# Cached sliding-window attention: twelve instead of eight rows of each wo head on five DMA engines, and other code blocks on two engines

## The chip, the cores and the metric

The kernel runs on one core of one Trainium2 chip. Its time is the device time of one execution in microseconds (us). Besides the plain runs there is one execution under the hardware profiler, whose span, from the first to the last instruction of the program, is a little shorter than the time reported for it.

## The reference

One decoding step of grouped-query attention over the last 512 positions of a cache: 32 batch rows, 32 query heads on 8 key/value heads, head size 128, bf16.

```python
W = min(4096, max(256, Sk // 4))                     # 512
q = (x @ wq).reshape(B, Sq, Hq, Dh)                  # x 32x512, wq 512x4096
k = jnp.repeat(k_cache[:, :, Sk - W:, :], rep, axis=1)
v = jnp.repeat(v_cache[:, :, Sk - W:, :], rep, axis=1)
scores = jnp.einsum("bhqd,bhkd->bhqk", q, k) * (Dh ** -0.5)
o = jnp.einsum("bhqk,bhkd->bhqd", softmax(scores), v)
out = o.reshape(B, Sq, Hq * Dh) @ wo                 # wo 4096x512
```

The window of K and that of V are 33.6 MB each, wq and wo 4.2 MB each: 75.5 MB in all, each byte read once.

## The kernel before, in words

**Tiling.** The 32 batch rows are taken in 8 quads of 4. A quad's K is one transfer of 4 MB into `K_sb[q % 2]` (128 partitions, one for each batch row, key/value head and quarter of the window; 32 KB each), its V the same into `V_sb[q % 2]`, for the last three quads in two pieces. `wq` is first loaded into `V_sb[1]`. At the end most of `wo` goes into `K_sb[0]`.

**wo in two parts.** The output projection is a sum over 32 heads of 128 rows each. The first `4 * NI` = 120 rows of every head are laid out over 128 partitions (32 heads by 4 groups of `NI` = 30 rows) and loaded by the steps W0, W1 and W2 of `LOADS` (line 269), 20, 8 and 2 rows of each partition at a time (`WOP`); each such transfer is carried by all sixteen DMA engines, eight partitions each. The last `NX` = 8 rows of every head go, one head to a partition, into another tile, `wx_row`, which lies over `QT_sb`. These are the steps A0 to A3 (line 262): 20, 5, 5 and 2 heads (`HEADS`), as transfers whose outer size is 5, 5, 5 and 2, and that many engines carry them. A head of A is 8 KB; a partition of W0, W1 and W2 is 20, 8 and 2 KB.

**The order of the work** is written out by hand: `PE_OPS`, `DVE_OPS` and `ACT_OPS` list the steps of TensorE, VectorE and ScalarE, `LOADS` those of the SP queue, and each step waits for the ends that `needs` gives. SP issues all large loads in one order, K and V of the quads in turn, then A0 to A3, then W0 to W2, then half of the store. A load of K waits until the transposes of the quad two before (T) are done, a load of V until the matmuls of the quad two before (P) are done with that part, A for the step Z0, W for T6.1.

**The steps of a quad.** T turns K into `KT_sb` on VectorE (L491), in two halves w = 0 and 1. S are the score matmuls (L353) with `QBD`, a block-diagonal copy of the queries, as weights. GpSimd makes `QBD` for a quad in four copies (L312), one of the two buffers at a time, after S of the quad two before. M and N (VectorE) and X (ScalarE) are the softmax. E (L368) spreads the probabilities over rows by matmuls with selectors `E_sb`, one 128 x 128 selector for each of 16 combinations, which GpSimd fills at the start in four copies (L301). G and B build the weights `bd` of P, the 128 matmuls with V (L383). C evicts their result into `C_sb`. F (L395, weights `F_sb`) and H (L404, weights `F_ext`) sort it into rows for the projection: F for the first 120 rows of each head, evicted by D (ScalarE, L561) into `o_sel`, H for the last eight, evicted by U (L566) into `o_ext`. `F_sb` and `F_ext` are zeroed by GpSimd and filled by VectorE in eight small copies (L471, L474) at the start.

**Z0** (ScalarE, L572) writes zeros over `wx_row` before A loads into it, since only 32 of its 64 partitions get a head.

**The end.** After D7 TensorE does the matmuls of W0 (20 x 4, L421), those of the head rows (8 x 4, L435), W1 and W2. VectorE and ScalarE each evict half of the result, and SP and ScalarE store it.

**Where the code lies.** TensorE's program has a directive ahead of its first matmul (line 320, `addr_align(256, offset=178)`): the next instruction stands at slot 178 of a block of 256 instructions, and the slots skipped are filled with instructions that do nothing. No other engine has one.

Of the kernel before, what the change touches and what calls it, by code (L numbers as in the profile page):

```python
# [5 lines left out]
BF16 = mybir.dt.bfloat16  # L6
# [14 lines left out]
P2.12.32 F2 H2 S4.0 S4.1 P3.0.12 E4 P3.12.32 S5.0 S5.1 S6.0 P4.0.4 E5 P4.4.8 S6.1 P4.8.24 E6 P4.24.32  # L21
F3 H3 S7.0 P5.0.20 S7.1 P5.20.32 E7 F4 H4 P6.0.32 F5 H5 P7.0.32 F6 H6 F7 H7
"""
# [6 lines left out]
X0 X1 G0 B0.4.8 G1 B1.4.8 C0.0.4 D0 U0 X2 G2 B2.4.8 C1.0.4 D1 U1 X3 G3 B3.4.8 C2.0.4 D2 U2 X4 G4 B4.4.8  # L30
C3.0.2 X5 G5 B5.4.8 X6 G6 C4.0.2 B6.4.7 D3 U3 B6.7.8 Z0 X7 C5.0.2 G7 B7.5.6 D4 U4 B7.6.8 C6.0.2 D5 U5 C7.0.2
D6 U6 D7 U7
"""
# [6 lines left out]
V_PIECES = 5 * [[0, 32]] + 2 * [[0, 16, 32]] + [[0, 18, 32]]  # L40
WOP = [(0, 20), (20, 28), (28, 30)]
HEADS = [(0, 20, 4, 0), (20, 25, 1, 32), (25, 30, 1, 33), (30, 32, 1, 34)]


# [4 lines left out]
def bass_standalone__sliding_block_cached__sampling_kernel(  # L49
# [15 lines left out]
    P = 128  # L65
# [4 lines left out]
    R = W // KB  # L70
    NI = 30
    NX = DH - 4 * NI
# [57 lines left out]
    with ExitStack() as es:  # L130
# [17 lines left out]
        F_ext = sb("F_ext", [P, 64], F32)  # L148
        E_sb = sb("E_sb", [P, KB, REP, 32, KB], BF16)
        F_sb = sb("F_sb", [P, 4, HQ, 4], F32)  # L150
        mask = sb("mask", [P, HKV], F32)
# [7 lines left out]
        wo_sb = K_sb[0][:, 0:NI * D].rearrange("p (i n) -> p i n", i=NI)  # L159
        wx_row = QT_sb[0:64].rearrange("p j w h t -> p (j w h t)")  # L160
        wx_sb = wx_row.rearrange("p (i n) -> p i n", i=NX)
# [10 lines left out]
        m_red = spare[:, 1856:1920].bitcast(F32)  # L172
        out_sb = P_bf[0:64, 0:256].rearrange("p (c n) -> p c n", c=2)
        Q_row = KT_sb[:, 0].rearrange("p r c t -> p (r c t)")[:, 0:HD]

# [3 lines left out]
        def folds(q):  # L179
# [10 lines left out]
            "pe_xT pe_q pe_Y dve_xT dve_q dve_QT dve_m dve_r dve_c act_q act_warm out_y "  # L190
            "pool_x pool_e pool_ei pool_q pool_f pool_m pool_j pool_qbd pool_fz"
        ).split()
# [10 lines left out]
        for b0, b1 in X_PARTS:  # L203
# [5 lines left out]
            V_sb[1][:, :], wq.rearrange("(p k) n -> p (k n)", k=DKT)  # L209
        ).then_inc(sem_wq, 16)  # L210
        regions = es.enter_context(ExitStack())
        block = regions.enter_context(nc.Block())
# [26 lines left out]
        def _(sp):  # L239
# [3 lines left out]
            for op in ops_of(" ".join(LOADS)):  # L243
# [14 lines left out]
                elif kind == "A":  # L258
                    wait([ends["Z", 0]])
                    h0, h1, k, p0 = HEADS[q]  # L260
                    n = (h1 - h0) // k
                    sp.dma_start(  # L262
                        wx_row[p0:p0 + 4 * n:1 if k == 4 else 4, :],
                        wo_h[h0:h1, 4 * NI * D:].rearrange("(k j) m -> j k m", k=k),
                    ).then_inc(sem_wx, 16)
                else:
                    wait([ends["T", NQ - 2, 1]])
                    i0, i1 = WOP[q]
                    sp.dma_start(  # L269
                        wo_sb[:, i0:i1, :].rearrange("p i n -> p (i n)"),  # L270
                        wo_r[:, :, i0 * D:i1 * D],
                    ).then_inc(sem_wo[q], 16)
# [3 lines left out]
        def _(pool):  # L276
            wait = Waits(pool)

            def diag(t, pattern, name):
# [11 lines left out]
            diag(m_id[:, :, :, :], [[-32, 4], [-4, HKV], [-1, KB]], "pool_m")  # L291
            pool.memset(F_sb[:, :, :, :], 0.0).then_inc(s["pool_fz"], 1)
            pool.memset(F_ext[:, :], 0.0).then_inc(s["pool_fz"], 1)

            diag(E_id[:, :, :].rearrange("p e (b h) -> p e b h", b=4),
                 [[-1, REP], [-4, 4], [-16, HKV]], "pool_ei")
            pool.memset(E_sb[:, :, :, :, :], 0.0).then_inc(s["pool_e"], 1)
            pool.wait_ge(s["pool_e"], 1)
            pool.wait_ge(s["pool_ei"], 2)
            for k in range(KB):  # L300
                pool.tensor_copy(E_sb[:, k, :, :, k], E_id[:, :, :]).then_inc(s["pool_e"], 1)  # L301
            pool.wait_ge(s["pool_e"], 5)
            pool.wait_ge(s["pool_q"], 1)
            pool.wait_ge(s["dve_QT"], 1)
            for q in range(NQ):
                if q >= 2:
                    wait([ends["S", q - 2, 1]])
                for b in range(4):
                    pr = slice(32 * b, 32 * b + 32)
                    if q or b:  # L310
                        pool.wait_ge(s["pool_qbd"], 4 * q + b)
                    pool.tensor_copy(  # L312
                        QBD[pr, q % 2].rearrange("p (w t) (h c) -> p w t h c", w=2, h=HKV)[
                            :, :, :, :, 4 * b:4 * b + 4],
                        QT_sb[pr, q].rearrange("p w (h e) t -> p w t h e", h=HKV),
                    ).then_inc(s["pool_qbd"], 1)

        @block.tensor
        def _(pe):
            pe.addr_align(256, offset=178)  # L320
            wait = Waits(pe)
# [20 lines left out]
            def scores(q, w):  # L342
                if w == 0:
                    pe.wait_ge(s["pool_qbd"], 4 * q + 4)
                if q == 0 and w == 0:
# [64 lines left out]
            for op in orders["PE"]:  # L410
                wait(needs(op))
                run[op[0]](*op[1:]).then_inc(op_sem["PE", op[0]], 1)
            wait([ends["D", NQ - 1]])
            for j, (i0, i1) in enumerate(WOP):
                pe.wait_ge(sem_wo[j], 16)
                last = j == len(WOP) - 1
                for cs in ((0, 1), (2, 3)) if last else (range(4),):
                    for i in range(i0, i1):
                        for c in cs:
                            n = 2 * (c % 2) + c // 2  # L420
                            ins = pe.matmul(  # L421
                                Y_ps[32 * c:32 * (c + 1), 0:P],
                                lhsT=o_sel[:, i, :],
                                rhs=wo_sb[:, i, n * P:(n + 1) * P],
                                start=i == 0, stop=i == NI - 1, tile_position=(0, 32 * c),
                            )
                    if last:
                        ins.then_inc(s["pe_Y"], 1)
                if j == 0:
                    wait([ends["U", NQ - 1]])  # L430
                    pe.wait_ge(sem_wx, 16 * len(HEADS))
                    for i in range(NX):
                        for c in range(4):
                            n = 2 * (c % 2) + c // 2
                            pe.matmul(  # L435
                                Y_ps[32 * c:32 * (c + 1), 0:P],
                                lhsT=o_ext[:, i, :],
                                rhs=wx_sb[:, i, n * P:(n + 1) * P],
                                start=False, stop=False, tile_position=(0, 32 * c),
                            )  # L440

# [8 lines left out]
        def _(dve):  # L450
# [27 lines left out]
            for n in range(4):  # L478
# [48 lines left out]
        def _(act):  # L527
# [41 lines left out]

            def zero(_):  # L570
                act.wait_ge(s["pool_qbd"], 4 * NQ)
                return act.activation(  # L572
                    wx_row, junk[0:64, 0:1].to_broadcast([64, NX * D]), ACTF.Copy
                )
# [40 lines left out]
```

## Time and profile before

| | us |
|---|---|
| plain runs, median of 3 (lowest to highest) | 184.67 (184.37 to 184.73) |
| the profiled execution, its own time | 184.59 |
| its span | 183.3 |
| VectorE busy, share of the span | 106.7, 58% |
| TensorE matmuls busy, share of the span | 120.4, 66% |
| ScalarE busy | 54.2, 30% |
| GpSimd busy | 17.1, 9% |
| mean rate of all DMA over the span | 414 GB/s |
| mean granted TensorE clock | 0.842 of full speed |

How to read it: the page names an engine, a source line and tiles ("out<-in") for each group of instructions, and for the DMA the queue. q1 is the queue of SP's loads, q10 that of ScalarE's, q8 and q14 bring instructions. "Busy" of a DMA queue is the time that its packets took, as a share of sixteen engines over the span. The chain of work that ended last is followed back from the last instruction, at each step to what released it. The trace behind the page also holds every DMA packet (queue, start, length, bytes), and every increment of a semaphore by a DMA engine; a transfer over sixteen engines makes sixteen of these as its engines finish.

### The profile page before, as it was taken

The numbers are of one execution on the slowest core, as the hardware profiler recorded it, in microseconds if no ns is written. First come the engines' busy times: TensorE is split into PE (matmuls) and PEld (weight loads), VectorE is DVE, ScalarE is ACT, GpSimd is POOL, SyncE is SP. The second block draws the span as 40 slices with busy tenths as digits, with TensorE's granted clock in tenths as the row PEclk, the third lists the DMA queues.
The fourth block names the chain that finished last, engine by engine and source line by source line (L and its number), as shares of the span: only waits on it lengthen the run. The fifth ranks groups of instructions, "written<-read, shape, count | busy, mean of one in ns | idle before, by whom it ended". The sixth has DMA issues, their size and how long they took to land.

```text
span 183.3 us, 3870 instructions
## 1 busy us (share of the span) xinstructions
PE 120.4 (66%) x1676; PEld 58.0 (32%) x1676; DVE 106.7 (58%) x109; ACT 54.2 (30%) x101; POOL 17.1 (9%) x53
## 2 busy tenths in 40 slices
PE   0029802416779699429944995440799978999984
PEld 0013300002535344304520252000255433655463
DVE  0042399998569534973289326999825994703030
ACT  3001300010590527501650135001053693803040
POOL 7900013020200020002000200001000000000000
PEclk9999995555769999996995599655559999999999
DMA  6998999989999999999999999999999999999981
GB/s 234 459 443 386 429 458 454 422 386 451 458 443 383 429 454 447 415 401 451 442 429 415 424 442 440 408 429 451 436 408 404 426 426 429 432 418 427 436 359 62
DMA packets 3517, 75.80 MB, mean 414 GB/s; under 512 B 429, under 2 KB 525, under 8 KB 653
## 3 DMA queue, kind: packets, MB, share of 16 engines
q1 hardware_dynamic: 3409, 75.52, 96.5%
q8 instruction: 13, 0.21, 0.5%
q10 hardware_dynamic: 92, 0.05, 0.1%
q14 instruction: 3, 0.02, 0.0%
HBM read 75.53 MB, written 0.03 MB: 412 GB/s over the span
## 4 chain that ended last, share of the span: by engine, by line
DMA 65%; DVE 19%; PE 8%; issue 4%; SPq 3%; ACT 0%; DVEq 0%
DMA K_sb<-in_k_cache_dram 32%; DVE KT_sb L491 16%; DMA V_sb<-in_v_cache_dram 16%; DMA K_sb<-in_wo_dram 11%; DMA V_sb<-in_wq_dram 7%; PE ps L336 5%; PE ps L383 2%; DVE QT_sb L483 2%; SPq L262 2%; SPq L255 1%; PE ps L421 1%; PE ps L353 1%; DVE C_sb L516 0%; SPq L269 0%; ACT KT_sb L533 0%
## 5 line engine op out<-in xcount | busy, mean ns | idle before, releaser
L491 DVE STREAM_TRANSPOSE KT_sb<-K_sb 128x4096 f32<-128x4096 f32 x16 | 70.5, 4430 | 7.2 <-DMA K_sb<-in_k_cache_dram 7.1
L383 PE MATMUL ps<-V_sb,bd 32*128 32x512 bf16 x1024 | 64.0, 402 | 4.4 <-DMA V_sb<-in_v_cache_dram 2.1
L353 PE MATMUL ps<-KT_sb,QBD 128*32 128x512 bf16 x256 | 24.7, 522 | 35.2 <-DVE KT_sb L491 26.0
L383 PEld LDWEIGHTS ps<-V_sb,bd 32*128 32x128 bf16 x1024 | 27.7, 98 | 37.8 <-issue 14.1
L353 PEld LDWEIGHTS ps<-KT_sb,QBD 128*32 128x32 bf16 x256 | 6.4, 111 | 50.4 <-DVE KT_sb L491 31.3
L539 ACT ACTIVATE P_f<-ps,negmax 128x512 f32<-128x512 f32 x8 | 5.5, 687 | 56.8 <-DVE negmax L499 56.8
L557 ACT ACTIVATE C_sb<-ps 32x512 f32<-32x512 f32 x22 | 12.9, 588 | 24.4 <-PE ps L383 24.2
L552 ACT ACTIVATE bd<-PTc,mask 128x512 bf16<-128x512 bf16 x31 | 20.1, 712 | 0.3
L312 POOL COPY QBD<-QT_sb 32x128 bf16<-32x128 bf16 x32 | 9.3, 289 | 106.3 <-PE ps L353 87.2
L511 DVE TENSOR_SCALAR bd<-PTc,mask 128x512 bf16<-128x512 bf16 x33 | 9.4, 349 | 14.0 <-ACT PTc L546 14.0
L516 DVE COPY C_sb<-ps 32x512 f32<-32x512 f32 x10 | 6.9, 693 | 13.9 <-PE ps L383 13.8
L395 PE MATMUL ps<-C_sb,F_sb 128*128 128x120 f32 x64 | 9.2, 286 | 6.8 <-ACT C_sb L557 6.5
L497 DVE TENSOR_REDUCE maxv<-ps 128x1 f32<-128x512 f32 x8 | 5.5, 687 | 10.8 <-PE ps L353 10.7
L395 PEld LDWEIGHTS ps<-C_sb,F_sb 128*128 128x128 f32 x64 | 7.7, 191 | 9.6 <-ACT C_sb L557 8.4
L368 PE MATMUL ps<-P_bf,E_sb 128*128 128x128 bf16 x128 | 9.9, 239 | 1.0 <-DVE P_bf L505 1.0
L336 PE MATMUL ps<-V_sb,bd 128*128 128x512 bf16 x32 | 9.0, 451 | 2.0 <-DMA V_sb<-in_wq_dram 2.0
L546 ACT ACTIVATE PTc<-ps 128x512 bf16<-128x512 f32 x8 | 4.7, 593 | 18.3 <-PE ps L368 18.3
L368 PEld LDWEIGHTS ps<-P_bf,E_sb 128*128 128x128 bf16 x128 | 8.4, 108 | 4.9 <-DVE P_bf L505 2.8
L325 PE MATMUL ps<-bd 32*128 32x128 bf16 x4 | 0.6, 298 | 10.5 <-DMA bd<-in_x_dram 10.5
L533 ACT ACTIVATE KT_sb<-ps 128x512 bf16<-128x512 f32 x4 | 2.4, 597 | 17.0 <-PE ps L336 17.0
L453 DVE CAST bd<-ps 128x512 bf16<-128x512 f32 x1 | 0.7, 692 | 11.2 <-PE ps L325 11.2
L480 DVE CAST KT_sb<-ps 128x512 bf16<-128x512 f32 x4 | 2.8, 692 | 6.0 <-PE ps L336 6.0
(37 smaller groups left out, 44.1 us busy)
## 6 DMA issues: line engine op xcount, KB each, us to landing
K_sb<-in_k_cache_dram SPq DMA_DIRECT2D x8, 4096.0 KB, 24.6
V_sb<-in_v_cache_dram SPq DMA_DIRECT2D x5, 4096.0 KB, 28.7
V_sb<-in_v_cache_dram SPq DMA_DIRECT2D x4, 2048.0 KB, 20.6
V_sb<-in_wq_dram SPq DMA_DIRECT2D x1, 4096.0 KB, 12.3
K_sb<-in_wo_dram SPq DMA_DIRECT2D x1, 2560.0 KB, 17.6
V_sb<-in_v_cache_dram SPq DMA_DIRECT2D x1, 2304.0 KB, 14.2
V_sb<-in_v_cache_dram SPq DMA_DIRECT2D x1, 1792.0 KB, 14.9
K_sb<-in_wo_dram SPq DMA_DIRECT2D x1, 1024.0 KB, 19.4
```

Of the source, the lines that this page charges most:

```text
L312: pool.tensor_copy(QBD[pr, q % 2].rearrange("p (w t) (h c) -> p w t h c", w=2, h=HKV)[:, :, :, :, 4 * b:4 * b + 4], QT_sb[pr, q].rearrange ...
L336: ins = pe.matmul(ps[:, n], lhsT=xT_sb[:, kt, :], rhs=wq_sb[:, kt, n * 512:(n + 1) * 512], start=kt == 0, stop=kt == DKT - 1, tile_positio ...
L353: ins = pe.matmul(S_ps[32 * c:32 * c + 32, :], lhsT=QBD[:, q % 2, 2 * w + t, c0:c0 + 32], rhs=KT_sb[:, w, :, KB * h:KB * h + KB, t], start ...
L368: ins = pe.matmul(EP_ps[:, e * R:(e + 1) * R], lhsT=E_sb[:, k, e].rearrange("p m j -> p (m j)"), rhs=P_bf[:, k * R:(k + 1) * R], start=k = ...
L383: ins = pe.matmul(O_ps[:, b, :], lhsT=bd[pr, q % 2, 4 * g:4 * g + 4].rearrange("p r h e -> p (r h e)"), rhs=V_sb[q % 2][pr, 512 * g:512 * ...
L395: ins = pe.matmul(folds(q), lhsT=F_sb[:, d].rearrange("p h d -> p (h d)"), rhs=C_sb[:, q % 2, :, NI * d:NI * d + NI], start=d == 0, stop=d ...
L491: return dve.transpose(KT_sb[:, w].bitcast(F32).rearrange("p r c t -> p r (c t)"), K_sb[q % 2][:, :].bitcast(F32).rearrange("p (r w c) -> ...
L497: dve.tensor_reduce(maxv[:, q:q + 1], S_ps, AX.X, ALU.max).then_inc(s["dve_m"], 1)
L511: ins = dve.tensor_scalar(o, i, m, None, op0=ALU.mult)
L516: ins = dve.tensor_copy(*pick_args(q, r))
L552: ins = act.activation(o, i, ACTF.Copy, scale=m)
L557: ins = act.activation(*pick_args(q, r), ACTF.Copy)
```

## The change

- `NI` goes from 30 to 29, and so `NX` from 8 to 12: W0, W1 and W2 carry 19, 8 and 2 rows of each partition, A0 to A3 twelve rows (12 KB) of each head. The transfers' outer sizes stay.
- `wx_row` lies over the first half of `KT_sb`. Z0 is gone from ScalarE; GpSimd zeroes `wx_row` in a memset after S7.0, the last reader of that half, and A waits for this.
- GpSimd makes `QBD` for two quads at once, in four copies of twice the size, after S of the quad before the two. `E_sb` holds one selector of 33 columns for each of 4 instead of 16 combinations, read at shifted places; GpSimd fills it in one copy. Filling `F_sb` and `F_ext` moves from VectorE to GpSimd (one copy and three), which waits for the reduction that makes `F_hd`. GpSimd's program goes from 75 to 59 instructions, VectorE's from 135 to 127 with the new directive.
- VectorE has a directive ahead of its part of the block: its next instruction stands at the start of a block of 128 slots, and it branches over the slots skipped. TensorE's directive has offset 154 instead of 178.
- In the order, H7 comes before F7 and U6 and U7 before D6 and D7. TensorE does the head rows' 48 matmuls first, after U7 and A, and then, after D7, those of W0, W1 and W2 (76, 32 and 8).

```diff
@@ -19,7 +19,7 @@
...
-F3 H3 S7.0 P5.0.20 S7.1 P5.20.32 E7 F4 H4 P6.0.32 F5 H5 P7.0.32 F6 H6 F7 H7
+F3 H3 S7.0 P5.0.20 S7.1 P5.20.32 E7 F4 H4 P6.0.32 F5 H5 P7.0.32 F6 H6 H7 F7
...
-C3.0.2 X5 G5 B5.4.8 X6 G6 C4.0.2 B6.4.7 D3 U3 B6.7.8 Z0 X7 C5.0.2 G7 B7.5.6 D4 U4 B7.6.8 C6.0.2 D5 U5 C7.0.2
-D6 U6 D7 U7
+C3.0.2 X5 G5 B5.4.8 X6 G6 C4.0.2 B6.4.7 D3 U3 B6.7.8 X7 C5.0.2 G7 B7.5.6 D4 U4 B7.6.8 C6.0.2 D5 U5 C7.0.2
+U6 D6 U7 D7
...
-WOP = [(0, 20), (20, 28), (28, 30)]
+WOP = [(0, 19), (19, 27), (27, 29)]
 HEADS = [(0, 20, 4, 0), (20, 25, 1, 32), (25, 30, 1, 33), (30, 32, 1, 34)]
+PICKS = [(0, 20, 4, 0), (20, 30, 2, 32), (30, 32, 1, 34)]
...
-    NI = 30
+    NI = 29
...
-        E_sb = sb("E_sb", [P, KB, REP, 32, KB], BF16)
-        F_sb = sb("F_sb", [P, 4, HQ, 4], F32)
+        E_sb = sb("E_sb", [P, REP, 33, KB], BF16)
+        F_pad = sb("F_pad", [P, 4 * (4 * HQ + 1)], F32)
...
-        wx_row = QT_sb[0:64].rearrange("p j w h t -> p (j w h t)")
+        wx_row = KT_sb[0:64, 0].rearrange("p r c t -> p (r c t)")[:, 0:NX * D]
...
+        F_sb = F_pad[:, 0:16 * HQ].rearrange("p (d h c) -> p d h c", d=4, h=HQ)
+        F_diag = F_pad[:, :].rearrange("p (d m) -> p d m", d=4)[:, :, 0:4 * HQ].rearrange(
+            "p d (h c) -> p d h c", c=4)[:, :, :, 0]
...
+        nc.vector.addr_align(128, offset=0, max_nops=0)
...
-                    wait([ends["Z", 0]])
+                    sp.wait_ge(s["pool_z"], 1)
...
-            pool.memset(F_sb[:, :, :, :], 0.0).then_inc(s["pool_fz"], 1)
+            pool.memset(F_pad[:, :], 0.0).then_inc(s["pool_fz"], 1)
...
-            pool.memset(E_sb[:, :, :, :, :], 0.0).then_inc(s["pool_e"], 1)
+            pool.memset(E_sb[:, :, :, :], 0.0).then_inc(s["pool_e"], 1)
             pool.wait_ge(s["pool_e"], 1)
             pool.wait_ge(s["pool_ei"], 2)
-            for k in range(KB):
-                pool.tensor_copy(E_sb[:, k, :, :, k], E_id[:, :, :]).then_inc(s["pool_e"], 1)
-            pool.wait_ge(s["pool_e"], 5)
+            pool.tensor_copy(E_sb[:, :, 0:32, KB - 1], E_id[:, :, :]).then_inc(s["pool_e"], 1)
+            pool.wait_ge(s["pool_e"], 2)
+            pool.wait_ge(s["pool_fz"], 2)
+            pool.wait_ge(s["dve_c"], 1)
+            pool.tensor_copy(
+                F_diag, F_hd.unsqueeze(1).to_broadcast([P, 4, HQ])
+            ).then_inc(s["pool_fz"], 1)
+            for h0, h1, k, p0 in PICKS:
+                n = (h1 - h0) // k
+                pool.tensor_copy(
+                    F_ext[:, p0:p0 + 4 * n].rearrange("p (j k) -> p k j", k=4)[:, 0:k],
+                    F_hd[:, h0:h1].rearrange("p (k j) -> p k j", k=k),
+                ).then_inc(s["pool_fz"], 1)
             pool.wait_ge(s["pool_q"], 1)
             pool.wait_ge(s["dve_QT"], 1)
-            for q in range(NQ):
-                if q >= 2:
-                    wait([ends["S", q - 2, 1]])
+            for q in range(0, NQ, 2):
+                if q:
+                    wait([ends["S", q - 1, 1]])
                 for b in range(4):
                     pr = slice(32 * b, 32 * b + 32)
                     if q or b:
-                        pool.wait_ge(s["pool_qbd"], 4 * q + b)
+                        pool.wait_ge(s["pool_qbd"], 2 * q + b)
                     pool.tensor_copy(
-                        QBD[pr, q % 2].rearrange("p (w t) (h c) -> p w t h c", w=2, h=HKV)[
-                            :, :, :, :, 4 * b:4 * b + 4],
-                        QT_sb[pr, q].rearrange("p w (h e) t -> p w t h e", h=HKV),
+                        QBD[pr].rearrange("p u a (h c) -> p u a h c", h=HKV).rearrange(
+                            "p u (w t) h c -> p (u w) t h c", w=2)[:, :, :, :, 4 * b:4 * b + 4],
+                        QT_sb[pr, q:q + 2].rearrange("p u w (h e) t -> p (u w) t h e", h=HKV),
                     ).then_inc(s["pool_qbd"], 1)
+            wait([ends["S", NQ - 1, 0]])
+            pool.memset(wx_row, 0.0).then_inc(s["pool_z"], 1)
...
-            pe.addr_align(256, offset=178)
+            pe.addr_align(256, offset=154)
...
-                    pe.wait_ge(s["pool_qbd"], 4 * q + 4)
+                    pe.wait_ge(s["pool_qbd"], 4 * (q // 2) + 4)
...
-                    pe.wait_ge(s["pool_e"], 5)
+                    pe.wait_ge(s["pool_e"], 2)
                 for e in range(REP):
+                    window = E_sb[:, e].rearrange("p m j -> p (m j)")
                     for k in range(KB):
                         ins = pe.matmul(
                             EP_ps[:, e * R:(e + 1) * R],
-                            lhsT=E_sb[:, k, e].rearrange("p m j -> p (m j)"),
+                            lhsT=window[:, KB - 1 - k:KB - 1 - k + P],
...
-                    pe.wait_ge(s["dve_c"], 7 + len(HEADS))
+                    pe.wait_ge(s["pool_fz"], 3 + len(PICKS))
...
+            wait([ends["U", NQ - 1]])
+            pe.wait_ge(sem_wx, 16 * len(HEADS))
+
...
+            for i in range(NX):
+                projected(o_ext[:, i, :], wx_sb[:, i], range(4), first=i == 0)
             wait([ends["D", NQ - 1]])
...
-                if j == 0:
-                    wait([ends["U", NQ - 1]])
-                    pe.wait_ge(sem_wx, 16 * len(HEADS))
-                    for i in range(NX):
...
 
...
-            dve.wait_ge(s["pool_fz"], 2)
...
-            for d in range(4):
-                dve.tensor_copy(F_sb[:, d, :, d], F_hd[:, :]).then_inc(s["dve_c"], 1)
-            for h0, h1, k, p0 in HEADS:
-                n = (h1 - h0) // k
-                dve.tensor_copy(
-                    F_ext[:, p0:p0 + 4 * n].rearrange("p (j k) -> p k j", k=4)[:, 0:k],
-                    F_hd[:, h0:h1].rearrange("p (k j) -> p k j", k=k),
-                ).then_inc(s["dve_c"], 1)
...
-            def zero(_):
-                act.wait_ge(s["pool_qbd"], 4 * NQ)
-                return act.activation(
-                    wx_row, junk[0:64, 0:1].to_broadcast([64, NX * D]), ACTF.Copy
-                )
-
             run = {"X": exponential, "G": gather, "B": spread, "C": pick, "D": folded,
-                   "U": folded_ext, "Z": zero}
+                   "U": folded_ext}
```

More of the change, by code (lines that the diff above doesn't have):

```diff
@@ L190, in bass_standalone__sliding_block_cached__sampling_kernel @@
             "pe_xT pe_q pe_Y dve_xT dve_q dve_QT dve_m dve_r dve_c act_q act_warm out_y "
-            "pool_x pool_e pool_ei pool_q pool_f pool_m pool_j pool_qbd pool_fz"
+            "pool_x pool_e pool_ei pool_q pool_f pool_m pool_j pool_qbd pool_fz pool_z"
         ).split()
@@ L412, in _, with projected @@
                 run[op[0]](*op[1:]).then_inc(op_sem["PE", op[0]], 1)
+            wait([ends["U", NQ - 1]])
+            pe.wait_ge(sem_wx, 16 * len(HEADS))
+            def projected(lhsT, rhs, cs, first=False, last=False):
+                for c in cs:
+                    n = 2 * (c % 2) + c // 2
+                    ins = pe.matmul(
+                        Y_ps[32 * c:32 * (c + 1), 0:P],
+                        lhsT=lhsT, rhs=rhs[:, n * P:(n + 1) * P],
+                        start=first, stop=last, tile_position=(0, 32 * c),
+                    )
+                return ins
+            for i in range(NX):
+                projected(o_ext[:, i, :], wx_sb[:, i], range(4), first=i == 0)
             wait([ends["D", NQ - 1]])
@@ L418, in _ @@
                     for i in range(i0, i1):
[L419 to L425, printed above, removed]
-                            )
+                        ins = projected(o_sel[:, i, :], wo_sb[:, i], cs, last=i == NI - 1)
                     if last:
                         ins.then_inc(s["pe_Y"], 1)
-                if j == 0:
-                    wait([ends["U", NQ - 1]])
-                    pe.wait_ge(sem_wx, 16 * len(HEADS))
-                    for i in range(NX):
[L433 to L440, printed above, removed]
         def spread_args(q, h):
@@ L568, in folded_ext @@
                     EP_ps[0:64, 0:4 * NX].rearrange("p (b i) -> p i b", b=4), ACTF.Copy)
-            def zero(_):
-                act.wait_ge(s["pool_qbd"], 4 * NQ)
-                return act.activation(
-                    wx_row, junk[0:64, 0:1].to_broadcast([64, NX * D]), ACTF.Copy
-                )
             run = {"X": exponential, "G": gather, "B": spread, "C": pick, "D": folded,
-                   "U": folded_ext, "Z": zero}
+                   "U": folded_ext}
             for op in orders["ACT"]:
```

## The prediction

> **What bounds the kernel now.** I read the DMA rows of the page first, then the busy time by stretches, the chain that ended last, and the timeline of the end.
>
> ```profile
> span 183.3 us, 3870 instructions
> ...
> q1 hardware_dynamic: 3409, 75.52, 96.5%
> q8 instruction: 13, 0.21, 0.5%
> ...
> q14 instruction: 3, 0.02, 0.0%
> ```
>
> The data queue fills 96.5% of sixteen engines' time; code loading shares the same engines: 13 pieces on q8, 3 on q14 (16 KB and 8 KB each, by the packet records). The columns of the next view are stretch, length, PE, PEld, DVE, ACT, POOL busy, PE clock, DMA share, GB/s:
>
> ```profile
> 2.00:172.00 170.00, 112.32 (x1460) 52.46 (x1464) 105.06 (x106) 51.98 (x94) 15.87 (x46) 0.83 1.00 427
> ...
> 178.00:179.00 1.00, 1.00 (x76) 1.00 (x80) 0.00 (x0) 0.00 (x0) 0.00 (x0) 1.00 0.64 262
> 179.00:180.00 1.00, 0.82 (x52) 0.54 (x40) 0.00 (x0) 0.00 (x0) 0.00 (x0) 1.00 0.46 168
> 180.00:181.00 1.00, 0.68 (x36) 0.51 (x40) 0.00 (x0) 0.00 (x0) 0.00 (x0) 1.00 0.04 16
> ```
>
> From 2 to 172 us the share is 1.00: no engine ever starves. Only in the last 4 us do engines run dry, one by one. So the end is set by the one engine with the most work, bytes and code both.
>
> ```profile
> 160.86 19.41 DMA K_sb<-in_wo_dram
> 180.27 0.04 issue
> 180.32 1.00 PE ps L421 x40
> ```
>
> The chain ends on the last `wo` transfers; 1.0 us of matmuls, one eviction and the store follow.
>
> **Which engine is last.** The trace has, for each transfer, one semaphore increment per engine that carries it. The last V piece, the last before the head rows, lands at 168.22, .26, .32, .47, .54, .86, .97, 169.41, .78, .80, .83, .95, 170.20, 171.26, .35, .38; the last `wo` piece at 177.41, .54, .76, 178.98, .99, 179.02, .13, .34, .84, .95, 180.31, .45, .47, .54, .58, .90. Between them lie 9.19 us of W packets (8 of 0.7615, 8 of 0.311, 8 of 0.0775). The 17 increments of the head rows (L262) come 0.31 us apart in five strings, beginning 1.24 us (four 8 KB packets) after 168.26, .47, .86, .97 and 169.41; the strings from .47 and .97 have one packet more, so those are the two engines that the two-head transfer uses. With 6 or 7 packets of 0.311 the low five end at 179.34, 179.84, 179.95, 180.31 and about 180.46, as recorded. The last, 180.90, is one of the other eleven, hit by a 16 KB code piece at 172.0 (started at 170.20, about 1.5 late).
>
> Three of the low five were late before the head rows: by 0.4, 0.5 and 1.0 against 168.2 to 168.5. The packet records show why: after each 8 KB code piece (87.65, 100.83, 108.06) one 1.213 us packet takes 1.875, 1.594 and 1.566, so a piece costs 0.97, 0.69 and 0.67 with its own 0.31. Followed by phase, they are the engines of 169.41 (piece at 87.65), 168.97 (100.83) and 168.86 (108.06). Whose code? Code pieces on q8 come 1 to 4 us after TensorE passes a block; by that lag the first fits VectorE's instruction 59 to 64, the second ScalarE's 60 to 62, the third GpSimd's 62 to 67. ScalarE's thus sits on a seven-packet engine.
>
> **The change, part by part.**
>
> *Rows moved.* 20 KB packets take 0.7615, 18 KB 0.6895, so 19 KB 0.7255: each of sixteen engines gets 8 x 0.036 = 0.29 less. 8 KB take 0.3105, 14 KB 0.5355, 16 KB 0.614; so 12 KB is estimated at 0.46, between 0.44 and 0.49. Six packets more by 0.15 are +0.90, seven +1.05. Net: low five +0.61 or, on two of them, +0.76; the other eleven -0.29.
>
> *Code.* GpSimd goes from 75 instructions to 59, under the 62 at which its piece was asked for: 0.67 less on the engine of 168.86. VectorE jumps to a block of 128 right after the start and has about 122 left, so its piece is asked for at about 0.7 us, before the first packets at 1.8: between 0 and 0.97; I take 0, nearest to the empty engines at that time. ScalarE loses one instruction, after its crossing: its 0.69 stays. TensorE's alignment moves from 178 to 154 and 24 instructions come at the end, so its 13 pieces stay, each some 0.5 us later.
>
> *Ends by engine*: 179.34 + 0.61 = 179.95; 179.84 + 0.76 = 180.60; 179.95 + 0.61 - 0.67 = 179.89; 180.31 + 0.76 = **181.07**; 180.46 + 0.61 - 0.97 = 180.10; the eleven at most 180.90 - 0.29 = 180.61. Last: 181.07, the ScalarE engine, +0.17.
>
> *Zeroing.* ScalarE's 3.60 us (148.2 to 151.8) becomes a GpSimd memset of 64 x 6144 after S7.0, which ended at 146.4.
>
> ```profile
> 148.21 3.60 ACT L572 ACTIVATE QT_sb<-junk 64x4096 bf16<-64x4096 f32 x1
> ...
> 157.10 3.06 SPq L262 DMA_DIRECT2D QT_sb<-in_wo_dram  x4
> 160.21 1.89 SPq L269 DMA_DIRECT2D K_sb<-in_wo_dram  x3
> ```
>
> 128 x 2048 took GpSimd 1.80, so 5.4, done at 151.9. SP is busy with V7.1 until 157.1; three W issues stand behind A, and SP's queue is full until 168. Cover 5 us; without it, nothing until A is later than about 166.
>
> *GpSimd's start.* Four double QBD copies instead of eight take 2.7 again (26.7 to 29.4); S0.0 begins at 31.06 behind a transpose: cover 1.6. Later pairs are copied one S earlier or later than needed: the last after S5.1 (123.4 to 126.1), S6.0 starts at 128.3. The fold masks (0.83 on VectorE at 12.5, GpSimd now, 0.2 to 1.5) have until 62.7. The shifted selector's matmuls (1.07 per group) could take up to twice that; P7 waits for V7.1 until 171.4, so about 1 us is free.
>
> *The end on TensorE.* H7 goes before F7, then 48 head-row matmuls (32 took 0.63: 0.95) and 76 (80 took 1.30: 1.24).
>
> ```profile
> 177.62 0.19 ACT L566 ACTIVATE o_ext<-ps 64x32 bf16<-64x32 f32 x1
> ...
> 177.96 1.30 PE L421 MATMUL ps<-K_sb,o_sel 128*32 128x128 bf16 x80 [0.38 <-DMA K_sb<-in_wo_dram]
> 179.19 0.63 PE L435 MATMUL ps<-QT_sb,o_ext 64*32 64x128 bf16 x32
> ```
>
> From F7's end at 177.6 that is done at 179.84; the second W transfer lands at 179.69 + 0.76 = 180.45. 0.6 us are free, and behind the last landing the same 0.4 us to the eviction follows: nothing.
>
> Sum: 183.3 + 0.17 = 183.47 of span, plus the 1.29 us around it, against the profiled execution's 184.59: 184.76. That execution is 0.08 under the median 184.67, so runs should lie near 184.8.
>
> **A rule weighed.** Row: 8 KB of code costs a full engine 0.67 to 0.97. [...]
>
> **The rivals.**
>
> *ScalarE's piece is not on the last engine* (it is the one at 108.06, and VectorE's or GpSimd's the one at 100.83). Then that engine ends at 181.07 - 0.69 = 180.38, and the end is 180.61: -0.29, 184.3 by the profiled run, 184.4 by the median. For it: ScalarE also waits at 104.6, 3.5 before that piece. Against: it needs VectorE to cross at 70, ScalarE at 65 and GpSimd at 60, where one place near 62 fits all three. With 12 KB packets at 0.44 a little more.
>
> *The jump loads two blocks, late*: pieces after the jump that land among the first loads cost their engine 2 x 0.97 instead of 0.97. Then 180.10 + 1.94 = 182.04: +1.14, 185.8. It decides once two pieces cost over 0.97 together. Against: first packets start at 1.8, the jump at 0.7.
>
> *The memset holds VectorE.* If T7.1 (146.75, 4.45 long) must wait until 151.9, it ends at 156.35 instead of 151.2; S7.1 starts at 156.4 instead of 152.7, P6, P7, and D7 follow 3.7 later, and less the 0.6 free at the end the time is +3.0, 187.6. It decides from 2.5 us on T7.1 (1.5 before S7.1, 1.0 later). Against: transposes beside the QBD copies took 4.45 against 4.40. [...]
>
> **How the numbers follow.** 0.2% is 0.37 us, about what a measurement of this kernel can tell from no change: bounds 184.30 and 185.04. Forecast, 50%: 184.8, own range 184.55 to 185.15 (12 KB at 0.44 to 0.49: +-0.2; ScalarE's piece at 0.97 instead of 0.69: +0.28); 0.15 of it over 185.04. First rival 29%, of which 0.14 under 184.30. Second 12%, third 9%, both slower. Faster 0.14, same 0.35 + 0.15 = 0.50, slower 0.15 + 0.12 + 0.09 = 0.36. The range goes from 184.2 to 185.5, leaving out most of the third rival and half of the second.
>
> **What would show it.** q14 with one piece in mid-run, near 100.8; one early. A's packets at 0.46. Last `wo` increments: eleven engines 0.29 earlier, one low engine alone near 181.1. The DMA share at 180 to 181 near 0.05 to 0.1. A issue still at 157. Wrong if two q14 pieces stay, if the last increment is below 180.7, or if TensorE rather than a landing ends the chain.

## The result and the profile after

| | before | after |
|---|---|---|
| plain runs, median (lowest to highest), 15 runs each | 184.50 (184.22 to 184.74) | 184.91 (184.69 to 185.18) |
| the profiled execution, its own time | 184.59 | 184.77 |
| its span | 183.3 | 183.5 |
| last `wo` increment in it | 180.90 | 181.09 |

The ratio is 1.0021, with a 95% interval of 1.0014 to 1.0028: the kernel became 0.41 us slower by the medians, and 0.18 us slower from one profiled execution to the other. The forecast was 184.8.

The DMA rows of the page of after:

```profile
span 183.5 us, 3845 instructions
...
q1 hardware_dynamic: 3409, 75.52, 96.4%
q8 instruction: 13, 0.21, 0.5%
...
q14 instruction: 2, 0.02, 0.0%
```

One of q14's three pieces is gone. The packet records put the two that stay at 3.69 and 100.87 us (before: 87.65, 100.83 and 108.06): GpSimd's is gone, ScalarE's is where it was, and VectorE's has moved to the start. The thirteen 16 KB pieces of q8 are TensorE's by the count of its instruction records: from its directive on they reach a multiple of 256 slots thirteen times, and a piece starts 1.1 to 5.2 us after each (before: 0.5 to 3.7).

The stretches of after; the columns are stretch, length, PE, PEld, DVE, ACT and POOL busy, PE clock, DMA share, GB/s:

```profile
2.00:172.00 170.00, 113.95 (x1464) 53.72 (x1468) 104.80 (x98) 48.56 (x93) 16.64 (x32) 0.81 1.00 427
178.00:179.00 1.00, 1.00 (x77) 0.90 (x68) 0.00 (x0) 0.00 (x0) 0.00 (x0) 1.00 0.59 244
179.00:180.00 1.00, 0.51 (x39) 0.34 (x25) 0.00 (x0) 0.00 (x0) 0.00 (x0) 1.00 0.44 164
180.00:181.00 1.00, 0.49 (x32) 0.46 (x32) 0.00 (x0) 0.00 (x0) 0.00 (x0) 1.00 0.06 25
```

The share is 1.00 up to 172 us as before, and it is still 0.06 in the last microsecond before the end: few of the sixteen engines still work then. The clock of this execution was 0.81 between 2 and 172 us against 0.83, with no consequence: TensorE is not what ends last, as the chain shows.

```profile
159.82 20.64 DMA K_sb<-in_wo_dram
180.46 0.04 issue
180.51 1.00 PE ps L437 x40
181.50 0.02 issue
181.53 0.27 ACT P_bf L581
```

The chain has the same form as before: it waits for a `wo` transfer, here W1, until 180.46 instead of 180.27, and the same 1.0 us of matmuls follows. W2 lands 0.63 us behind W1 on the engine that is last, so the last increments of W2 are used below to compare engines.

The increments of the last `wo` transfer, one for each of the sixteen engines:

```
before  177.41 177.54 177.76 178.98 178.99 179.02 179.13 179.34 179.84 179.95 180.31 180.45 180.47 180.54 180.58 180.90
after   177.10 177.21 177.68 178.55 178.74 178.79 179.10 179.91 179.96 180.03 180.05 180.09 180.12 180.29 180.83 181.09
```

In after three of the five engines with head rows end last, at 180.29, 180.83 and 181.09. They are known by their strings of A's increments, which now come 0.46 apart (0.31 before). The engine of 181.09 has a string of four (170.81, 171.28, 171.74, 172.20), so it carried seven packets, and its V7.1 landed at 168.97 against 168.2 to 168.3 of the undisturbed ones: it is the one that ScalarE's piece had hit. The engine of 180.83 has a string of three (171.02, 171.48, 171.94) and landed V7.1 at 169.18: it is VectorE's.

### The profile page after: what moved, and what is told of

It reads as the page before. It is cut to its first block, busy times and chain, and to the rows that moved or that the text cites. A ratio compares the mean times of both kernels' runs of the same rounds, so it can differ in the third digit from the quotient of the medians.

```text
span 183.5 us, 3845 instructions
## 1 busy us (share of the span) xinstructions
PE 122.0 (67%) x1688; PEld 59.3 (32%) x1688; DVE 106.5 (58%) x101; ACT 50.9 (28%) x100; POOL 17.9 (10%) x39
## 4 chain that ended last, share of the span: by engine, by line
DMA 65%; DVE 18%; PE 8%; issue 5%; SPq 3%; ACT 0%; DVEq 0%
DMA K_sb<-in_k_cache_dram 31%; DMA V_sb<-in_v_cache_dram 15%; DVE KT_sb L496 15%; DMA K_sb<-in_wo_dram 11%; DMA V_sb<-in_wq_dram 7%; PE ps L353 5%; PE ps L401 2%; DVE QT_sb L488 2%; SPq L267 2%; SPq L260 1%; PE ps L437 1%; PE ps L370 1%; DVE C_sb L521 0%; SPq L274 0%; ACT KT_sb L538 0%
## 5 line engine op out<-in xcount | busy, mean ns | idle before, releaser
L401 PE MATMUL ps<-V_sb,bd 32*128 32x512 bf16 x1024 | 61.7, 390 | 4.0 <-DMA V_sb<-in_v_cache_dram 1.8
L370 PE MATMUL ps<-KT_sb,QBD 128*32 128x512 bf16 x256 | 26.1, 547 | 33.6 <-DVE KT_sb L496 24.4
L401 PEld LDWEIGHTS ps<-V_sb,bd 32*128 32x128 bf16 x1024 | 26.7, 95 | 36.5 <-issue 11.6
L327 POOL COPY QBD<-QT_sb 32x256 bf16<-32x256 bf16 x16 | 6.2, 389 | 106.1 <-PE ps L370 90.6
L413 PE MATMUL ps<-C_sb,F_pad 128*128 128x116 f32 x64 | 10.9, 322 | 6.5 <-ACT C_sb L562 6.5
L413 PEld LDWEIGHTS ps<-C_sb,F_pad 128*128 128x128 f32 x64 | 9.4, 225 | 9.3 <-ACT C_sb L562 8.0
L353 PE MATMUL ps<-V_sb,bd 128*128 128x512 bf16 x32 | 9.5, 469 | 2.7 <-DMA V_sb<-in_wq_dram 2.7
L333 POOL MEMSET KT_sb<- 64x6144 bf16 x1 | 5.2, 5211 | 21.4 <-PE ps L370 21.4
```

Of the source, the lines that this page charges most:

```text
L327: pool.tensor_copy(QBD[pr].rearrange("p u a (h c) -> p u a h c", h=HKV).rearrange("p u (w t) h c -> p (u w) t h c", w=2)[:, :, :, :, 4 * b ...
L353: ins = pe.matmul(ps[:, n], lhsT=xT_sb[:, kt, :], rhs=wq_sb[:, kt, n * 512:(n + 1) * 512], start=kt == 0, stop=kt == DKT - 1, tile_positio ...
L370: ins = pe.matmul(S_ps[32 * c:32 * c + 32, :], lhsT=QBD[:, q % 2, 2 * w + t, c0:c0 + 32], rhs=KT_sb[:, w, :, KB * h:KB * h + KB, t], start ...
L401: ins = pe.matmul(O_ps[:, b, :], lhsT=bd[pr, q % 2, 4 * g:4 * g + 4].rearrange("p r h e -> p (r h e)"), rhs=V_sb[q % 2][pr, 512 * g:512 * ...
L413: ins = pe.matmul(folds(q), lhsT=F_sb[:, d].rearrange("p h d -> p (h d)"), rhs=C_sb[:, q % 2, :, NI * d:NI * d + NI], start=d == 0, stop=d ...
```

## The experiments

In each run the kernel before was timed on the same chip in turn: 184.51 (35 runs) beside after once more, eight rows, no jump and eight engines; 184.44 (22) beside the last two heads as two transfers, the second execution of eight engines, the same without the jump, and before once more; 184.49 (14) beside sixteen rows and six engines.

**After once more.** No edit; it gives the spread that the other runs are read against.

> The changed kernel once more, beside before. Last-engine theory (the end is set by the DMA engine with the most packets, here the one with seven head packets and ScalarE's code piece): last wo increment again near 181.1, 0.2 to 0.5 us slower than before. It says what the comparisons of this set are to be held against; both theories expect the same here.

184.86 median (184.79 to 185.06, 11 runs), 1.0017 with 1.0009 to 1.0026; the last increment at 181.12, q14's pieces at 3.84 and 100.86. The small loss is there again.

**Eight rows again, all else as after.** This undoes the moved rows alone; the jump, the shorter GpSimd program and the memset stay.

```diff
-WOP = [(0, 19), (19, 27), (27, 29)]
+WOP = [(0, 20), (20, 28), (28, 30)]
-    NI = 29
+    NI = 30
```

> The changed kernel with eight rows of each head on the five engines again (NI 30, 20/8/2 rows per W transfer); code, GpSimd's work, jump and order stay as changed. Last-engine theory: the seven-packet engine ends at about 180.3 and VectorE's at 180.2, the engines with two 16 KB code pieces at 180.4 to 180.9 are last again; time as before, within 0.15 us. Rival (the rearranged code, the memset or GpSimd's copies cost the time, the moved rows nothing): stays 0.4 us slower than before.

184.52 (184.28 to 184.61, 11 runs), ratio 0.9997 with 0.9989 to 1.0006: the time of before. Its last increment is at 180.88, on an engine without head rows (its V7.1 landed at 171.69, and 9.19 us of W packets follow), with 180.72, 180.66 and 180.63 close behind. The two engines hit by the 8 KB pieces were expected at about 180.3 and 180.2; their V7.1 landed at 169.28 and 169.47, which with their packets gives 180.65 and 180.53: later than expected, but still not last. So the loss is the moved rows' alone, and all that the change does to code and to GpSimd, taken together, is worth nothing: the engines that it frees are not the last.

**No jump on VectorE.** One directive is taken out of after.

```diff
-        nc.vector.addr_align(128, offset=0, max_nops=0)
```

> The changed kernel without VectorE's directive. Last-engine theory: VectorE's 8 KB code piece comes in mid-run again, near 88 us instead of 3.7, costs the same 0.7 to 1.0 us on the same engine, and ScalarE's engine stays the last: time as the changed kernel, within 0.1 us; wq lands 0.5 us earlier, which nothing at the end shows. Rival (the jump's early piece delays the start and with it all that follows): 0.4 to 0.5 us faster than the changed kernel.

184.97 (184.83 to 185.10, 11 runs), 1.0022 with 1.0014 to 1.0031. q14's pieces are now at 90.17 and 101.10, so the directive does move VectorE's piece. GpSimd's went with its shorter program, so the piece near 101 is ScalarE's by exclusion; no run takes that one away. The last increments are 181.32 and 181.20. The first matmuls with `wq` tell what the early piece does; after, and then without the jump:

```profile
13.68 1.87 PE L353 MATMUL ps<-V_sb,bd 128*128 128x512 bf16 x4 [2.71 <-DMA V_sb<-in_wq_dram]
```

```profile
13.13 2.29 PE L352 MATMUL ps<-V_sb,bd 128*128 128x512 bf16 x5 [1.85 <-DMA V_sb<-in_wq_dram]
```

With the jump, one engine's share of `wq` is late by about 0.5 us (its last increment is at 13.55 in after, 13.03 in before) and TensorE starts that much later. It costs nothing by itself, because the loads behind it keep the queue full (a share of 1.00 up to 172 us); but the engine that carried the piece is about as late at the end as if the piece had come in mid-run: it lands V7.1 at 169.18 to 169.53 in the eight executions with the jump, and at 169.34, 169.41 and 169.54 in three of the four without (in the fourth, before once more, three engines landed between 169.19 and 169.25). The jump neither costs nor gains: 184.97 and 184.86 are 0.1 apart with ranges that overlap.

**Sixteen rows on the same five engines.** One step further in the same direction tells a bound that changes hands from a cost in proportion.

```diff
-WOP = [(0, 19), (19, 27), (27, 29)]
+WOP = [(0, 18), (18, 26), (26, 28)]
-    NI = 29
+    NI = 28
```

> The kernel after with sixteen instead of twelve rows of each head on the five engines (16 KB packets at 0.614, W0 18 KB at 0.6895 of each partition). Last-engine theory: the step from eight to twelve rows cost little because the last engine changed from one of the eleven (180.88) to ScalarE's (181.09), and the step from twelve to sixteen pays in full on ScalarE's engine: seven packets by 0.151 is +1.06, W0 0.29 less, so its last increment is 181.86 and the time about 185.65 (+0.75 on after); the eleven end another 0.29 earlier, below 179.9. Rival, cost in proportion to the rows (packet handling, memset, matmuls): the same step as from eight to twelve rows, +0.35 to 0.4 by the medians, 185.2 to 185.3.

185.69 (185.61 to 185.90, 4 runs), 1.0068 with 1.0055 to 1.0081; last increment 181.99. Its chain:

```profile
159.61 21.75 DMA K_sb<-in_wo_dram
181.41 0.99 PE ps L437 x40
182.42 0.27 ACT P_bf L581
```

The last landing of W1, 180.46 in after, is at 181.41. From eight to twelve rows the last increment moved by 0.21 (180.88 to 181.09), from twelve to sixteen by 0.90, and the medians by 0.34 to 0.39 and by 0.78 to 0.83. Steps of one size that cost so differently are what the last-engine theory expects: in the first the last engine changes from one of the eleven to one of the five, in the second the same engine pays in full (+1.06 of packets, -0.29 of W0, +0.77; its V7.1 also landed 0.16 later, at 169.13 instead of 168.97). A cost in proportion to the rows falls. One number of the expectation missed: the eleven should have ended below 179.9, and the last of them is at 180.08.

**The last two heads as two transfers.** Meant to take a packet off ScalarE's engine, if a transfer of one head is carried by one engine.

```diff
-...V7.0 V7.1 A0 A1 A2 A3 W0 W1 W2
+...V7.0 V7.1 A0 A1 A2 A3 A4 W0 W1 W2
-HEADS = [(0, 20, 4, 0), (20, 25, 1, 32), (25, 30, 1, 33), (30, 32, 1, 34)]
+HEADS = [(0, 20, 4, 0), (20, 25, 1, 32), (25, 30, 1, 33), (30, 31, 1, 34), (31, 32, 1, 38)]
```

> The changed kernel with the transfer of the last two heads cut into two of one head each, which no outer size of two or five holds to two engines any more. Last-engine theory: if a one-head transfer is spread over all engines, ScalarE's engine loses one 12 KB packet (0.46) and VectorE's engine is last, at about 180.9 instead of 181.1: 0.2 us faster than the changed kernel. If a one-head transfer goes to one engine, that engine gets eight packets: 0.4 slower if it is ScalarE's, otherwise 0.2 faster. Rival (the packets on these engines do not set the end): no change.

185.00 (184.83 to 185.44, 10 runs), 1.0032 with 1.0023 to 1.0041: not faster. The packet records, linked by their starts and ends, show that both one-head transfers went to one and the same engine, which then had eight packets, and that ScalarE's had six. Yet the last increment was at 181.23, with two more at 181.18 and 181.10. On ScalarE's engine and on the one with eight packets the first 19 KB packet of W0 took 1.065 and 0.936 us instead of 0.7255, with no code piece there, so ScalarE's engine kept only 0.12 of the 0.46. And VectorE's engine, expected at about 180.9, was no earlier: its V7.1 landed at 169.49 instead of 169.18, which with its packets gives 181.18. Why the two packets were long stays open.

**Eight engines instead of five.** Here eight engines carry four packets of 12 KB each, in one transfer.

```diff
-HEADS = [(0, 20, 4, 0), (20, 25, 1, 32), (25, 30, 1, 33), (30, 32, 1, 34)]
-PICKS = [(0, 20, 4, 0), (20, 30, 2, 32), (30, 32, 1, 34)]
+HEADS = [(0, 32, 4, 0)]
+PICKS = [(0, 32, 4, 0)]
```

> The changed kernel with the head rows as one transfer of all 32 heads with outer size 8, so on eight engines with four 12 KB packets each, instead of six or seven on five engines. Last-engine theory: each of the five loses 0.9 to 1.4 us, three idle engines get 1.8; the last of these eight ends near 179.9, the engines with two 16 KB code pieces are last at about 180.1; last increment 0.9 to 1.0 earlier, time 0.9 below the changed kernel and 0.5 below before. Rival (the time sits in code, memset or TensorE's end): time as the changed kernel.

The times fell into two groups: 184.24 to 184.52 (3 of 12) and 185.49 to 186.24 (9). The profiled execution, 184.24, is of the lower one, with a last increment at 180.57 against the 180.1 expected; no execution reached the time of about 184.0 that was forecast. A second profiled execution of the same kernel was taken for the other group.

> The kernel with all 32 heads in one transfer over eight engines, a second look: its times fell into two groups, 184.2 to 184.5 and 185.5 to 186.2, and the look taken was of the first. Last-engine theory: in an execution of the second group one engine's last wo increment lies 1.2 to 1.6 us behind 180.6, because a 16 KB code piece came ahead of its last packets (a third piece on one engine). Rival (TensorE waits for its own code or for a landing of the head rows): the increments end at 180.6 as before and TensorE's last matmuls are late all the same.

This execution took 185.78 us. Its last increments are 182.10 and, next, 180.43: one engine alone is late. TensorE's matmuls at the end, in this execution:

```profile
179.15 1.24 PE L437 MATMUL ps<-K_sb,o_sel 128*32 128x128 bf16 x76 [0.52 <-DMA K_sb<-in_wo_dram]
181.51 0.94 PE L437 MATMUL ps<-K_sb,o_sel 128*32 128x128 bf16 x40 [1.11 <-DMA K_sb<-in_wo_dram]
```

Against the lower group's execution:

```profile
180.00 0.92 PE L437 MATMUL ps<-K_sb,o_sel 128*32 128x128 bf16 x40 [0.27 <-DMA K_sb<-in_wo_dram]
```

The late engine was late at V7.1 already. In this execution the landings of V7.1 stand in groups: 168.26 to 168.90, then 169.22 and 169.53 (the engines of the two 8 KB pieces), five at 169.65 to 170.22 and three at 171.33 to 171.53. Eleven 16 KB pieces of TensorE's code had come by then, and one piece for each of the five and two for each of the three make eleven. From 171.33, four packets of A (1.85) and the W packets (8.91) lead to 182.1. That the pieces fell so is read from the times, since the packet records do not name the engine. So an engine with head rows got two pieces here. In the lower group's execution none did, since it would have ended near 182 there too; the last increment, 180.57, fits an engine with one piece (169.83, and the same 1.85 and 8.91). After has eight engines free of TensorE's code, the five with head rows and three that end below 178 (177.10, 177.21, 177.68). Here too eight are free of it by their landings of V7.1, but in both executions only two engines end below 178, so six of the eight with head rows are free of it and two are not. And which engines get a second piece differs between executions of one kernel. I had taken the three that are new here to be free of it; that was wrong.

**The same without the jump.** To see whether the jump makes the two groups.

```diff
-HEADS = [(0, 20, 4, 0), (20, 25, 1, 32), (25, 30, 1, 33), (30, 32, 1, 34)]
-PICKS = [(0, 20, 4, 0), (20, 30, 2, 32), (30, 32, 1, 34)]
+HEADS = [(0, 32, 4, 0)]
+PICKS = [(0, 32, 4, 0)]
...
-        nc.vector.addr_align(128, offset=0, max_nops=0)
```

> All heads over eight engines, and no directive on VectorE. Last-engine theory: VectorE's piece moves to mid-run on an engine that has over 1 us to spare: times as with the directive, both groups. Rival (the early piece makes the two groups): one group, near 184.2.

Two groups again, 184.23 to 184.50 (7 of 12) and 185.67 to 186.00 (5). The jump does not make them.

**Six engines.** This asks whether one more engine can be had without TensorE's code, and takes a packet off ScalarE's engine without a one-head transfer.

```diff
-...V7.0 V7.1 A0 A1 A2 A3 W0 W1 W2
+...V7.0 V7.1 A0 A1 A2 W0 W1 W2
-HEADS = [(0, 20, 4, 0), (20, 25, 1, 32), (25, 30, 1, 33), (30, 32, 1, 34)]
-PICKS = [(0, 20, 4, 0), (20, 30, 2, 32), (30, 32, 1, 34)]
+HEADS = [(0, 24, 4, 0), (24, 30, 1, 32), (30, 32, 1, 33)]
+PICKS = HEADS
```

> [...] Rival: the loss of after comes from something other than the packets on one engine (smaller packets, more matmuls at the end); then the time is after's 184.9 in one group.

184.49 to 184.78 in five runs and 186.17 to 186.32 in four. The forecast was 184.3 to 184.4 for a sixth engine free of TensorE's code, and for one that has it two groups, near 184.5 and 186.2, an estimate from the second execution of eight engines: 180.43 and 182.10 with four packets, and 0.46 for a fifth, make 180.9 and 182.6 at the end. It is the second case. In the profiled execution, 184.60, the sixth engine has had one 16 KB piece, and its string (171.59, 172.05) leads to the last increment, 180.92. ScalarE's engine, with six packets, ends at 180.81 instead of 181.09 (0.46 less for the packet, 0.17 more because its V7.1 landed at 169.14 instead of 168.97), and VectorE's, with five, at about 180.51. So ScalarE's engine is last in after because of its seven packets: with six it no longer is. But the sixth engine is one of TensorE's. By their landings, the engines with head rows got none of TensorE's code in the eight executions profiled that have five of them. Three of the other eleven got none before V7.1 either; the transfers over six engines reached none of these three, and no run shows one that reaches them without an engine of TensorE's.

**Before once more.** A second profile of the kernel before, to see where its last landing lies from one execution to the next.

> The kernel before once more, for the spread of its last landing. Last-engine theory: the last wo increment is again of an engine with two 16 KB pieces or of ScalarE's, between 180.5 and 180.9, and the time of the execution less that increment is 3.7 as in the first profile.

184.54 us, with its last increments at 180.77, 180.67, 180.61, 180.57 and 180.57; the time less the last increment is 3.77. In before several engines stand close together at the end, and by their landings of V7.1 the last one was in both executions an engine hit by TensorE's piece at 172.0 and at 172.62 (in the second, 170.05 at V7.1, 9.19 of W packets and 1.5 for the piece make 180.74). No version tried was faster than before in all its executions.

## Why the prediction was right, and where it was not

**The last engine: right.** "181.07, the ScalarE engine" was measured as 181.09, with seven packets of 0.463 (0.46 estimated from the packets of 8, 14 and 16 KB). The two steps behind it were tested each by itself: sixteen rows push this engine by 0.90, one packet less (six engines) pulls it back to 180.81, under another. That the last increment sets the time is shown across all twelve profiled executions: they took 184.24 to 185.78 us, and the time less the last `wo` increment is 3.64 to 3.77 in every one. The agreement to 0.02 is luck: in the seven executions with seven packets on this engine its V7.1 landed between 168.97 and 169.28, and the sum took 168.97 from the one profile of before. With the same packets it ended at 181.12 in after once more and at 181.32 without the jump.

**The ends of the others.** The eleven were put at 180.61 at most and ended at 180.12 in after; in before one of them was last through a code piece at 172.0, and in after none of the eleven was so late. The two profiled executions of before have their last landing at 180.90 and 180.77, so the bound held the end of one execution, not of the kernel.

**VectorE's early piece: wrong.** "Between 0 and 0.97; I take 0, nearest to the empty engines at that time." The piece came at 3.69 us, not at about 0.7, into a queue that was full already, and its engine ended at 180.83 instead of 180.10: 0.73, nearly the upper end. It did not show in the time only because 180.83 is under 181.09. The bound was right, the choice in it was not; the prediction had a row to go by, that q8's pieces come 1 to 4 us after their cause (0.5 to 3.7 by the count in before), which can put a piece asked for at 0.7 behind the first packets at 1.8.

**Code otherwise: right.** GpSimd's piece went, ScalarE's stayed at 100.87 and TensorE's thirteen pieces stayed. The kernel with eight rows shows what this is worth: nothing, since it frees engines that were not last.

**GpSimd and the zeroing: right, but VectorE was held for a moment.** From the timeline of after, the memset, T7.1 beside it, the spreading behind T7.1 (B6.0.4), and the issue of A:

```profile
146.51 5.21 POOL L333 MEMSET KT_sb<- 64x6144 bf16 x1 [21.36 <-PE ps L370]
...
146.79 4.45 DVE L496 STREAM_TRANSPOSE KT_sb<-K_sb 128x4096 f32<-128x4096 f32 x1
...
151.16 1.50 DVE L516 TENSOR_SCALAR bd<-PTc,mask 128x512 bf16<-128x512 bf16 x4
...
156.05 2.40 SPq L267 DMA_DIRECT2D KT_sb<-in_wo_dram  x3
```

The same spreading in before:

```profile
151.12 1.10 DVE L511 TENSOR_SCALAR bd<-PTc,mask 128x512 bf16<-128x512 bf16 x4
```

5.21 against 5.4 expected, done at 151.72; A is issued at 156.05 (157 expected), with 4.3 us of cover. The transpose beside the memset took the 4.45 that it takes alone, so the third rival, a transpose held until 151.9, did not come about.

But the spreading behind it, which overlaps the memset's last 0.56 us, took 1.50 for four instead of 1.10. The trace's single instructions show that the first of the four was held until the memset was done: it took 0.717 us instead of 0.314, and ended at 151.88. In after once more the memset ended at 152.19 and the first one at 152.34, after 1.084 us; with sixteen rows the memset ended at 153.22 and the first one at 153.38, after 2.417 us; with eight rows the memset ended at 149.95, before the spreading, and the first one took 0.314. So the rival's mechanism exists, on an instruction that the prediction did not look at. It cost nothing here: the maxima that follow it start at 152.77 (153.82 in before), and in all these runs a landing ends the chain.

The four `QBD` copies took 1.74 together (2.7 expected: a size that was wrong and did no harm), and the matmuls with the shifted selector 1.07 per group, in six of the eight groups, as before.

**The end on TensorE: right.** From the timeline of after:

```profile
177.49 0.85 PE L437 MATMUL ps<-KT_sb,o_ext 64*32 64x128 bf16 x48
178.27 1.25 PE L437 MATMUL ps<-K_sb,o_sel 128*32 128x128 bf16 x76
180.51 0.93 PE L437 MATMUL ps<-K_sb,o_sel 128*32 128x128 bf16 x40 [0.99 <-DMA K_sb<-in_wo_dram]
```

TensorE is done with the head rows and W0 at 179.52 (179.84 expected) and then waits 0.99 us for the landing, so the 16 matmuls more cost nothing.

**The size.** The sum gave +0.17 between profiled executions, and +0.18 was measured there. But the medians are 0.41 apart (0.26 to 0.52 by the interval), and the step that failed is the last one, "that execution is 0.08 under the median". Over 15 runs before's profiled execution lies 0.09 above the median, 184.50, and after's lies 0.14 under its own; 0.18, 0.09 and 0.14 make the 0.41. For before the second profile shows the size of it: the last landing at 180.77 instead of the 180.90 that the sum started from. For after the two executions profiled ended at 181.09 and 181.12; a time of 184.91 less the 3.68 that lie behind the last increment in after gives a last increment near 181.23 as an estimate, which is inside what the landings of V7.1 allow (the same kernel without the jump had 181.32). That this is the reason of the 0.14 is not shown, since plain runs leave no trace. That the forecast of 184.8 came within 0.11 of 184.91 is luck in part: it started from a median of three runs, 184.67, which is 0.17 above that of fifteen, and added about 0.1 where 0.41 was measured. The ratio, 1.0021, lies at the 0.2% that the text named as what can be told from no change, with its interval on both sides of it, and no rival had a part in it.

**The rivals.** ScalarE's piece off the last engine: no, 181.09 stands alone with ScalarE's lateness. Two blocks for the jump: no, one piece at 3.69. VectorE held by the memset through T7.1: no, only its next instruction, for 0.40 us.

**The rule weighed.** A piece of code is not free for the DMA engine that brings it, with its queue full: the packet records give 0.67 to 0.97 for 8 KB in before, and 1.50 to 1.58 for 16 KB (the piece's own 1.0 to 1.1 and 0.45 to 0.55 more on the packet behind it). Whether the engine that runs the code is held up was not measured here.

## What to carry to other kernels

Here the DMA engines were full up to 172 us (a share of 1.00) and the time was the work of one engine (3.64 to 3.77 us behind its last increment in twelve executions). In such a kernel count bytes and code pieces for each engine and look for the one that is last after the change: bytes moved from eleven engines to five paid nothing here once one of the five had become the last (181.09). Code counts as traffic, also at the start, where a piece that came at 3.69 to 4.06 us still delayed its engine by about as much as one in mid-run (V7.1 at 169.18 to 169.53, without the jump at 169.34 to 169.54). The memset on GpSimd held the instruction of VectorE that overlapped it until it ended (0.717 us instead of 0.314 in after), so look at the instruction behind the one that was checked. And take the base of a sum from several executions where engines stand close together at the end: one profile shows one draw.

## What was not expected of the hardware

- A piece of code asked for at about 0.7 us, by the prediction's estimate, came at 3.69 to 4.06 us and delayed its engine by 0.73 us at the end in after, although VectorE, whose code it was, had its first work only at 11 us.
- TensorE's 16 KB pieces come on eight engines, by the landings of V7.1: in each of the twelve executions eleven pieces had come by then, five engines landed at 169.59 to 170.34 (one piece) and three at 171.16 to 171.69 (two). Which engines get a second one differs between executions of the same kernel. With head rows on some of those eight, executions of one kernel differ by about 1.4 us (eight engines) or 1.6 us (six).
- GpSimd's memset held VectorE's tensor_scalar until it ended, up to 2.417 us instead of 0.314 with sixteen rows, while the transpose beside the memset took its usual 4.45 in after.
- With two one-head transfers in a row, single 19 KB packets took up to 1.065 us instead of 0.7255 on two engines. This was seen in one trace and not explained.
